# Convolution and two expert layers on one core: three blocks of tokens instead of two side by side in the first units

## The chip, the cores and the metric

The kernel runs on one core of a Trainium2 chip, in one launch. The metric is device time in microseconds (us), from the start to the end of the execution. Before the change the median of three runs is 2334.19 us (2333.78 to 2334.38). Engines: PE is TensorE (matmuls), DVE is VectorE, ACT is ScalarE, POOL is GpSimd, SP is SyncE, which here only issues DMAs.

## The reference

For 16384 tokens (4 sequences of 4096) of width 192, in float32:

```python
w = exp(weight - max) ; w = w / (sum(w) + 1e-9)      # 8 heads x 7 taps
out[b, s] = sum_k w[head, k] * x_pad[b, s + k]       # causal, 7 taps, 24 channels a head
h = maximum(out @ moe_w_in, 0); y1 = (h * h) @ moe_w_out        # 192 -> 2048 -> 192
h = y1 @ moe2_w_in; g = where(h > 0, h, exp(minimum(h, 0)) - 1); return g @ moe2_w_out
```

The weights of both layers come as float64 and are read as pairs of 32-bit words.

## The kernel before

**Blocks and units.** The tokens go in 32 blocks of 512 (TB). Layer 1 or 2 of a block is cut into 8 *units* of 256 hidden columns: `units` lists the 512 units as (layer, block, number). In the main loop, turn u issues the first products of unit u (`gemm1`: h, two PSUM banks) and the second products of unit u - 3 (`gemm2`, LAG = 3: they add to y, two banks, A for channels 0 to 127 and B for the other 64). Between them ACT takes `r` from h (`act_first`), squares it (layer 1) and rounds it to `gh`, and DVE (at some u POOL) computes the rest, `gl = r - gh` (`finish_lo`). Every operand is held as a high and a low part, so one logical product is three. `r` has two buffers, `gh` and `gl` three.

**Two forms of products.** From unit HALVES on, `products` issues the two halves of the array in turns (L458). Below it uses whole-array products (L471, L477): first those of h, then those of y.

**Order of the units.** `merge` lets layer 1 of block 0 begin at turn 0 and that of block 1 at turn 3, turn and turn about; then come layer 1 of blocks 2 and 3, layer 2 of blocks 0 and 1, and from there layer 2 of block j - 2 and layer 1 of block j. The first unit of block 1 is number 4, that of block 2 number 16.

**Weights.** A layer's weights are prepared in 18 pieces (`pieces`), each due at a unit. `piece_step` i ends piece i - 2 on POOL (`finish`), does the second part of piece i - 1 (DVE `power` and `rest`, POOL's sum) and the first part of piece i (ACT square, DVE `start`, `sign`, `guard`), and issues the load of a later piece, whose buffer `rest` has freed. So a step is five DVE operations (L178, L205, L189, L212, L200), and POOL does three or four for each piece. `more_pieces` makes up to two steps a unit as long as `begin[i] <= u`, with begin = due - 8 for layer 1.

**The convolution.** `place_x` brings a block into channel order: halo copies and two DVE transposes. For blocks 0 and 1 (`early`) the 7 taps are PE products with diagonal matrices (conv, 7 for half A of 512 columns, 7 for half B of 256; PE makes two passes of each), then `hi_a`, `hi_b` (ACT casts) and `lo_a`, `lo_b` (subtractions) make the four operand tiles X1[j]. For later blocks the taps are DVE operations (L349, L351). What isn't due at once stands in `bg`, from which `task` takes a few per unit, in order. All engines take their instructions in program order.

**PSUM.** `ps_h` has two buffers of two banks, `ps_y` four of one bank: two for y of each of two blocks; the early convolutions use `ps_y` too.

The pieces that the prediction's steps touch are `load_x`, `place_tasks`, `conv_tasks`, `gemm1`, `gemm2`, the list of units, and the block under `manual_schedule` ahead of the loop (the start).

Of the kernel before, what the change touches and what calls it, by code (L numbers as in the profile page):

```python
# [9 lines left out]
F32 = mybir.dt.float32  # L10
# [15 lines left out]

HALVES = 16

# [14 lines left out]
def conv_moe_moe_kernel(  # L43
# [39 lines left out]
    ev_p = ctx.enter_context(tc.tile_pool(name="ev", bufs=2))  # L83
    ps_h = ctx.enter_context(tc.tile_pool(name="ps_h", bufs=2, space=PSUM))
    ps_y = ctx.enter_context(tc.tile_pool(name="ps_y", bufs=4, space=PSUM))
# [24 lines left out]

    def softmax_taps():
# [149 lines left out]

    def load_x(j, second=nc.sync):
# [6 lines left out]
        def part(i, q):  # L269
            p = slice(q * Q, (q + 1) * Q)  # L270
            if i == 0:
                nc.sync.dma_start(out=a[p], in_=src[:, :, p])
            else:
                half, ch = q // 2, P + q % 2 * Q
                t = slice(half * (HB // Q), (half + 1) * (HB // Q))
                second.dma_start(out=b[p], in_=src[:, t, ch : ch + Q])
            if (i, q) == (1, P // Q - 1):
                xin[j] = (a, b)

        for i in range(2):  # L280
            for q in range(P // Q):
                later(lambda i=i, q=q: part(i, q))

    def place_tasks(j):
# [14 lines left out]
        def turn(i):  # L299
            while j not in xin:  # L300
                transfer()
            if i == 0:
                halo()
            t = xT[j][i]
            nc.vector.transpose(out=t[:, HALO:], in_=xin[j][i].rearrange("p t c -> p (t c)"))
            if i == 1:
                nc.vector.tensor_copy(out=t[DB:, 0:HALO], in_=t[0:DB, HB:])
                xin.pop(j)

# [3 lines left out]

        return [lambda: turn(0), lambda: turn(1), more]

# [21 lines left out]
    def conv_tasks(j, early=False):  # L337
        st = {}

        def tap(i, cw, k):  # L340
            t = xT[j][i]
            n = (TB, HB)[i]
            if early:
                if k == 0:
                    st[i] = ps_y.tile([P, TB], F32, tag="y", name=f"conv{i}")[:, 0:n]
                nc.tensor.matmul(st[i], diag(i, k), t[:, k : k + n], start=k == 0, stop=k == K - 1)  # L346
            elif k == 0:
                st[i] = acc_p.tile([P, n], F32, tag=f"acc{i}", name="acc")
                nc.vector.tensor_scalar(out=st[i], in0=t[:, 0:n], scalar1=cw[:, 0:1], scalar2=None, op0=ALU.mult)  # L349
            else:  # L350
                nc.vector.scalar_tensor_tensor(  # L351
                    out=st[i], in0=t[:, k : k + n], scalar=cw[:, k : k + 1], in1=st[i], op0=ALU.mult, op1=ALU.add
                )

        def hi_a():
            X1[j] = in_tiles("x1")
            nc.scalar.copy(out=X1[j][0], in_=st[0])

        def lo_a():
            eng = nc.gpsimd if j == 2 else nc.vector  # L360
            eng.tensor_tensor(out=X1[j][1], in0=st[0], in1=f32(X1[j][0]), op=ALU.subtract)
# [4 lines left out]
        def hi_b():  # L366
            for (p, n), (other, _) in zip(halves(), reversed(halves())):
                nc.scalar.copy(out=X1[j][2][p, n], in_=st[1][p, :])
                if j <= LEAD:
                    nc.scalar.copy(out=X1[j][2][other, n], in_=st[1][p, :])  # L370

        def lo_b():
# [3 lines left out]
            if j <= LEAD:  # L376
                for (p, n), (other, _) in zip(halves(), reversed(halves())):
                    nc.scalar.copy(out=l[other, n], in_=f32(l[p, n]))
                ready.add((1, j))
                return  # L380
# [11 lines left out]
        if early:  # L392
            return taps[0] + taps[1] + [hi_a, lo_a, hi_b, lo_b]
        return [t for both in zip(*taps) for t in both] + [hi_a, hi_b, lo_a, lo_b]
# [4 lines left out]

    def gemm1(W, X, i):  # L400


        h = ps_h.tile([P, 2, TB], F32, tag="h", name="h")
        work = {}
# [15 lines left out]
    def gemm2(layer, j, i, gh, gl):  # L420

        if i == 0:
            Y[layer, j] = [ps_y.tile([P, TB], F32, tag="y", name=f"y{layer}{s}") for s in "AB"]
        o = (W1 if layer == 1 else W2)["o"]
# [82 lines left out]
    def y1_tasks(j):  # L507
# [52 lines left out]

    units = merge((1, 0, 0, 1.0), (1, 1, LEAD, 1.0))
    phases = [(1, 2), (1, 3), (2, 0), (2, 1)]
    for j in range(4, NB):
# [48 lines left out]
    with tc.manual_schedule():  # L612
        nc.scalar.dma_start(out=taps[:, 0:K], in_=weight)
        load_piece()
        load_x(0, nc.scalar)
        for _ in range(2):
            load_piece()
        make_pick()
        diags.extend(in_tiles("x2", F32))
        make_identity(nc, diag(0, K))  # L620
        warm_up(4)
        softmax_taps()
        place_x(0)
        load_x(1)
        piece_step()
        spread_taps()
        warm_up(14)
        first, bg = conv_tasks(0, early=True), deque((0, t) for t in conv_tasks(1, early=True))
        for i, cw in enumerate((cwA, cwB)):
            make_diags(i, cw)  # L630
            for t in first[i * K : (i + 1) * K]:
                t()
            piece_step()
        place_x(1)
        load_x(2)
        for t in first[2 * K : 2 * K + 2]:
            t()
        piece_step()
        for t in first[2 * K + 2 :]:
# [22 lines left out]
        def next_x(l2, j2, c2):  # L662

            if (l2, j2) == (1, 1):
                return {0: 2, 3: 3}.get(c2)
            if l2 == 2 and c2 == 2 and j2 != 1:
                return 4 if j2 == 0 else j2 + 3 if j2 + 3 < NB else None

        for u in range(NU + LAG):
# [4 lines left out]
            if u < NU:  # L674
                layer, j, c = units[u]
                while (layer, j) not in ready:
                    bg.popleft()[1]() if bg else transfer()
                hs[u], first = gemm1(W1 if layer == 1 else W2, (X1 if layer == 1 else X2)[j], c)
            v = u - LAG
# [71 lines left out]
```

## Time and profile before

| | |
|---|---|
| median of 3 runs | 2334.19 us |
| profiled execution | 2334.18 us, its span 2332.5 us |
| PE busy | 2308.0 us, 19296 matmuls |
| DVE / ACT / POOL busy | 1720.6 / 1494.5 / 129.8 us |
| mean granted TensorE clock | 0.998 of full speed |
| HBM | 25.17 MB read, 12.58 MB written, 16 GB/s |

A busy PE is not PE at its peak, since matmuls overlap; where it waits is read from gaps and from the distance of the units. Of the 40 slices of the page PE shows less than 9 tenths only in the first and the last, and POOL works only in the first four: the weights are prepared there.

### The profile page before, as it was taken

The numbers are of one execution on the slowest core, as the hardware profiler recorded it, in microseconds if no ns is written. First come the engines' busy times: TensorE is split into PE (matmuls) and PEld (weight loads), VectorE is DVE, ScalarE is ACT, GpSimd is POOL, SyncE is SP. The second block draws the span as 40 slices with busy tenths as digits, with TensorE's granted clock in tenths as the row PEclk, the third lists the DMA queues.
The fourth block names the chain that finished last, engine by engine and source line by source line (L and its number), as shares of the span: only waits on it lengthen the run. The fifth ranks groups of instructions, "written<-read, shape, count | busy, mean of one in ns | idle before, by whom it ended". The sixth has DMA issues, their size and how long they took to land.

```text
span 2332.5 us, 46226 instructions
## 1 busy us (share of the span) xinstructions
PE 2308.0 (99%) x19296; PEld 2048.2 (88%) x19296; DVE 1720.6 (74%) x2032; ACT 1494.5 (64%) x1639; POOL 129.8 (6%) x149
## 2 busy tenths in 40 slices
PE   8899999999999999999999999999999999999998
PEld 6688998988998898888999899999989999988987
DVE  7978877767777777777777777677777777777665
ACT  5686756666666666666666666666666666666656
POOL 5465000000000000000000000000000000000000
PEclk9999999999999999999999999999999999999999
DMA  4211111000101000100001010001010001100000
GB/s 104 59 51 40 19 24 17 15 15 15 20 15 20 12 15 17 19 15 17 13 14 19 17 18 15 15 15 19 15 19 12 15 17 18 17 17 8 13 8 14
DMA packets 221342, 48.06 MB, mean 21 GB/s; under 512 B 206288, under 2 KB 219600, under 8 KB 221136
## 3 DMA queue, kind: packets, MB, share of 16 engines
q1 hardware_dynamic: 220032, 45.00, 10.1%
q8 instruction: 152, 2.49, 0.5%
q14 instruction: 54, 0.44, 0.1%
q10 hardware_dynamic: 1104, 0.13, 0.0%
HBM read 25.17 MB, written 12.58 MB: 16 GB/s over the span
## 4 chain that ended last, share of the span: by engine, by line
PE 94%; ACT 2%; DVE 2%; issue 1%; DMA 0%; POOL 0%; SPq 0%; DVEq 0%; ACTq 0%; POOLq 0%
PE h L458 43%; PE y2A L458 15%; PE y1A L458 14%; PE y1B L458 9%; PE y2B L458 9%; ACT gh L647 1%; DVE r L494 1%; ACT r L481 1%; PE h L471 1%; PE conv L346 1%; PE y1A L471 1%; ACT r L485 0%; PE h L477 0%; PE y1B L471 0%; DVE gl L653 0%
## 5 line engine op out<-in xcount | busy, mean ns | idle before, releaser
L647 ACT CAST gh<-r 128x1024 fp32r<-128x1024 f32 x512 | 538.1, 1051 | 632.9 <-DVE r L494 318.9
L653 DVE TENSOR_TENSOR gl<-r,gh 128x1024 fp32r<-128x1024 f32 x507 | 629.7, 1242 | 345.5 <-ACT gh L647 345.2
L481 ACT ACTIVATE r<-h 128x1024 f32<-128x1024 f32 x512 | 524.7, 1025 | 150.7 <-PE h L458 138.7
L458 PE MATMUL y2A<-gh,wo 64*128 64x512 f32 x2024 | 552.4, 392 | 0.0
L458 PE MATMUL y1A<-gh,wo 64*128 64x512 f32 x1944 | 531.2, 392 | 0.0
L494 DVE SCALAR_TENSOR_TENSOR r<-r,h 128x1024 f32<-128x1024 f32 x256 | 311.6, 1217 | 202.0 <-ACT r L485 176.5
L458 PEld LDWEIGHTS y2A<-gh,wo 64*128 64x128 f32 x2024 | 367.4, 184 | 21.7
L458 PEld LDWEIGHTS y1A<-gh,wo 64*128 64x128 f32 x1944 | 352.6, 184 | 13.1 <-issue 0.4
L458 PE MATMUL h<-x2Ah,wiAh 64*128 64x512 f32 x1024 | 326.4, 397 | 4.5 <-DVE r L494 4.5
L458 PE MATMUL h<-x2Al,wiAh 64*128 64x512 f32 x1024 | 323.2, 393 | 0.0
L458 PE MATMUL h<-x2Ah,wiAl 64*128 64x512 f32 x1024 | 322.1, 392 | 0.0
L458 PE MATMUL y2A<-gl,wo 64*128 64x512 f32 x1012 | 319.8, 395 | 0.0
L458 PE MATMUL y2B<-gh,wo 64*128 64x512 f32 x1012 | 314.2, 390 | 0.0
L458 PE MATMUL y2B<-gl,wo 64*96 64x512 f32 x1012 | 314.1, 390 | 0.0
L458 PE MATMUL y1A<-gl,wo 64*128 64x512 f32 x972 | 304.2, 392 | 0.0
L458 PE MATMUL h<-x1Ah,wiAh 64*128 64x512 f32 x960 | 302.7, 393 | 1.2 <-ACT r L481 1.2
L492 DVE SCALAR_TENSOR_TENSOR r<-h,r 128x1024 f32<-128x1024 f32 x224 | 272.6, 1217 | 41.8 <-ACT r L481 41.6
L458 PE MATMUL h<-x1Al,wiAh 64*128 64x512 f32 x960 | 302.7, 393 | 0.0
L458 PE MATMUL h<-x1Ah,wiAl 64*128 64x512 f32 x960 | 301.5, 391 | 0.0
L458 PE MATMUL y1B<-gh,wo 64*128 64x512 f32 x972 | 301.2, 389 | 0.0
L458 PE MATMUL y1B<-gl,wo 64*96 64x512 f32 x972 | 300.1, 388 | 0.4 <-POOL gl L653 0.4
L485 ACT ACTIVATE r<-r 128x1024 f32<-128x1024 f32 x256 | 271.6, 1061 | 8.1
(137 smaller groups left out, 4784.3 us busy)
## 6 DMA issues: line engine op xcount, KB each, us to landing
xinA<-in_x_dram SPq DMA_DIRECT2D x128, 64.0 KB, 2.2
out_dram<-zA SPq DMA_DIRECT2D x128, 64.0 KB, 2.0
raw<-in_moe_w_out_dram SPq DMA_DIRECT2D x16, 384.0 KB, 3.1
out_dram<-zB SPq DMA_DIRECT2D x64, 64.0 KB, 2.0
xinB<-in_x_dram SPq DMA_DIRECT2D x124, 32.0 KB, 1.9
x1Bh<-x1Bh SPq DMA_DIRECT2D x56, 64.0 KB, 1.9
x1Bl<-x1Bl SPq DMA_DIRECT2D x56, 64.0 KB, 1.9
raw<-in_moe_w_in_dram SPq DMA_DIRECT2D x8, 384.0 KB, 3.3
```

Source lines behind the costliest of these rows:

```text
L346: nc.tensor.matmul(st[i], diag(i, k), t[:, k : k + n], start=k == 0, stop=k == K - 1)
L458: m = nc.tensor.matmul(o, w[p], x[p], start=st, stop=sp)
L471: nc.tensor.matmul(o, w, x, start=st, stop=sp and part in ("A", "B"))
L481: nc.scalar.activation(out=r, in_=h, func=AF.Relu, scale=1.0 if layer == 1 else -1.0)
L485: nc.scalar.activation(out=r, in_=r, func=AF.Exp, scale=-1.0)
L492: nc.vector.scalar_tensor_tensor(out=r, in0=h, scalar=0.0, in1=r, op0=ALU.max, op1=ALU.mult)
L494: nc.vector.scalar_tensor_tensor(out=r, in0=r, scalar=-1.0, in1=h, op0=ALU.add, op1=ALU.max)
L647: nc.scalar.copy(out=gh, in_=gs[u])
L653: eng.tensor_tensor(out=gl, in0=gs.pop(u), in1=f32(gsplit[u][0]), op=ALU.subtract)
```

## The change

Three blocks are merged instead of two: block 0 begins at turn 0, block 1 at 2, block 2 at 4. So block 1's first unit is number 3, block 2's number 8, and blocks 0, 1 and 2 end layer 1 with units 15, 20 and 23. Three y need six banks: `ps_h` gets one buffer under each of two tags. Under tag "z" stand the convolution of block 0 and then y of block 0; until unit 19 (HALVES goes from 16 to 20) every h uses the one buffer "h", after that h alternates between the two. Block 2's convolution becomes PE products, and its operands use the second buffer of "x2". y of block 1 is taken up only after unit 23.

At the start the taps' softmax and x come ahead of the weights; half B is convolved before half A; two of x's eight loads go to ACT's queue; ACT's table is loaded early by a small exponential; the second warm-up has 8 products instead of 14.

```diff
-HALVES = 16
+HALVES = 20
...
-    ps_h = ctx.enter_context(tc.tile_pool(name="ps_h", bufs=2, space=PSUM))
+    ps_h = ctx.enter_context(tc.tile_pool(name="ps_h", bufs=1, space=PSUM))
...
+    def exp_table():
+        one = cpool.tile([H, 1], F32, name="one")
+        nc.vector.memset(one, 1.0)
+        nc.scalar.activation(out=one, in_=one, func=AF.Exp)
...
-        for i in range(2):
-            for q in range(P // Q):
-                later(lambda i=i, q=q: part(i, q))
+        for n, queue in enumerate(queues):
+            later(lambda i=1 - n // 4, q=n % 4, queue=queue: part(i, q, queue))
...
-        return [lambda: turn(0), lambda: turn(1), more]
+        return [lambda: turn(1), lambda: turn(0), more]
...
+        if early:
+            both = ps_h.tile([P, 2, TB], F32, tag="z", name="conv") if j == 0 else None
+            for i, n in enumerate((TB, HB)):
+                st[i] = (both[:, i] if j == 0 else ps_y.tile([P, TB], F32, tag="y", name=f"conv{i}"))[:, 0:n]
...
+        def begin_x1():
+            if j not in X1:
+                X1[j] = in_tiles("x2" if j == 2 else "x1")
...
-            return taps[0] + taps[1] + [hi_a, lo_a, hi_b, lo_b]
+            return taps[1] + [hi_b, lo_b] + taps[0] + [hi_a, lo_a]
...
-        h = ps_h.tile([P, 2, TB], F32, tag="h", name="h")
+        h = ps_h.tile([P, 2, TB], F32, tag=tag, name="h")
...
-            Y[layer, j] = [ps_y.tile([P, TB], F32, tag="y", name=f"y{layer}{s}") for s in "AB"]
+            if (layer, j) == (1, 0):
+                both = ps_h.tile([P, 2, TB], F32, tag="z", name="y10")
+                Y[layer, j] = [both[:, s] for s in range(2)]
+            else:
+                Y[layer, j] = [ps_y.tile([P, TB], F32, tag="y", name=f"y{layer}{s}") for s in "AB"]
...
+    def y1_from(j):
+
+        return at[1, 2, NP - 1] + 1 if j == 1 else 0
...
-    units = merge((1, 0, 0, 1.0), (1, 1, LEAD, 1.0))
-    phases = [(1, 2), (1, 3), (2, 0), (2, 1)]
+    units = merge((1, 0, 0, 1.0), (1, 1, 2, 1.0), (1, 2, 4, 1.0))
+    phases = [(1, 3), (2, 0), (2, 1)]
...
-        load_piece()
-        load_x(0, nc.scalar)
-        for _ in range(2):
-            load_piece()
+        exp_table()
+        softmax_taps()
+        load_x(0, (nc.sync,) * 6 + (nc.scalar,) * 2)
         make_pick()
         diags.extend(in_tiles("x2", F32))
         make_identity(nc, diag(0, K))
         warm_up(4)
-        softmax_taps()
+        for _ in range(3):
+            load_piece()
+        spread_taps()
         place_x(0)
         load_x(1)
...
+        warm_up(8)
+        for i, cw in ((1, cwB), (0, cwA)):
+            make_diags(i, cw)
+        first, bg = conv_tasks(0, early=True), deque()
+        later_x = conv_tasks(1, early=True) + place_tasks(2) + conv_tasks(2, early=True)
+        bg.extend((0, t) for t in later_x)
...
-                return {0: 2, 3: 3}.get(c2)
+                return {3: 3}.get(c2)
...
-                hs[u], first = gemm1(W1 if layer == 1 else W2, (X1 if layer == 1 else X2)[j], c)
+                hs[u], first = gemm1(W1 if layer == 1 else W2, (X1 if layer == 1 else X2)[j], c, "h" if u < HALVES or u % 2 else "z")
```

On PE, before, the second products of the first unit (y1A, y1B) are followed at once by the next unit's first products:

```order
L471 MATMUL y1B<-gh,wo_96 128x512 x2
L471 MATMUL y1B<-gl,wo_96 96x512 x2
L471 MATMUL h<-x1Ah,wiAh_92 128x512
L471 MATMUL h<-x1Ah,wiAl_93 128x512
L471 MATMUL h<-x1Al,wiAh_92 128x512
```

On PE, after, at the same place (y_455 is y of block 0 in the pair of banks, conv_199 the convolution of block 2's half B):

```order
L490 MATMUL y_455<-gh,wo_96 128x512 x2
L490 MATMUL y_455<-gl,wo_96 96x512 x2
L354 MATMUL conv_199<-xtB,x2Bh 128x256
L490 MATMUL h<-x1Ah,wiAh_92 128x512
L490 MATMUL h<-x1Ah,wiAl_93 128x512
```

A tap of block 2 now stands between the two, and it reads `xtB`, which DVE writes. On DVE, before, the third `gl` is followed by a piece step:

```order
L653 TENSOR_TENSOR gl<-r,gh 128x1024
L178 TENSOR_SCALAR a<-raw 128x384
L205 TENSOR_SCALAR m<-a 128x384
L189 SCALAR_TENSOR_TENSOR a<-raw,a 128x384
L212 SCALAR_TENSOR_TENSOR m<-raw,m 128x384
L200 SCALAR_TENSOR_TENSOR a<-m,a 128x384
```

On DVE, after, the placement of block 2 (halo copies, transposes) stands behind the third `gl`, ahead of the step:

```order
L680 TENSOR_TENSOR gl<-r,gh 128x1024
L299 COPY xtA<-xtA 128x6
L300 COPY xtB<-xtB 64x6
L309 STREAM_TRANSPOSE xtB<-xinB 128x256
L311 COPY xtB<-xtB 64x6
L309 STREAM_TRANSPOSE xtA<-xinA 128x512
L183 TENSOR_SCALAR a<-raw 128x384
```

That transpose is the one which the tap above reads. On DVE, after, between the sixth and seventh `gl` (first row) and the eighth to tenth (last row) stand a step and block 2's `lo_a`, `x2Al<-conv_198`:

```order
L680 TENSOR_TENSOR gl<-r,gh 128x1024 x2
L183 TENSOR_SCALAR a<-raw 128x384
L210 TENSOR_SCALAR m<-a 128x384
L194 SCALAR_TENSOR_TENSOR a<-raw,a 128x384
L217 SCALAR_TENSOR_TENSOR m<-raw,m 128x384
L205 SCALAR_TENSOR_TENSOR a<-m,a 128x384
L372 TENSOR_TENSOR x2Al<-conv_198,x2Ah 128x512
L680 TENSOR_TENSOR gl<-r,gh 128x1024 x3
```

This subtraction is what block 2's first unit, number 8, reads as its low part; before, block 2 had its taps and its subtractions later, ahead of unit 16.

## Rows read from the trace of the kernel before

**Rows 1.** The page, section 1: busy us (share), instructions.

```profile
PE 2308.0 (99%) x19296; PEld 2048.2 (88%) x19296; DVE 1720.6 (74%) x2032; ACT 1494.5 (64%) x1639; POOL 129.8 (6%) x149
```

**Rows 2.** Groups by line and form, ACT, 300 to 2300: busy us, mean ns, idle.

```profile
L481 ACT ACTIVATE r<-h 128x1024 f32<-128x1024 f32 x452 | 463.4, 1025 | 129.6 <-PE h L458 128.9
```

**Rows 3.** Busy time by window: PE, PEld, DVE, ACT, POOL, PE clock, DMA.

```profile
35.47:82.08 46.61, 38.34 (x163) 24.83 (x161) 46.52 (x65) 24.77 (x35) 35.49 (x38) 0.96 0.28 82
```

**Rows 4.** Waits of PE, 20 to 83: us in total, times, longest.

```profile
PE y1A L471 <- DVE gl L653: 5.2, 3, 2.4
```

**Rows 5.** Timeline of PE, 0 to 24: start us, us, line, tiles.

```profile
5.94 5.86 PE L335 MATMUL warm<-x2Al 128*128 128x128 f32 x28
...
20.49 0.58 PE L471 MATMUL h<-x1Ah,wiAh 128*128 128x512 f32 x1
...
23.78 0.49 PE L477 MATMUL h<-x1Bl,wiBh 64*128 64x512 f32 x2 [0.53 <-ACT x1Bl L378]
```

**Rows 6.** PE by window, block 0's A taps and B taps: length, busy.

```profile
11.64:17.65 6.01, 6.01 (x16) 1.00 0.45 119
17.65:20.49 2.84, 2.84 (x16) 1.00 0.68 108
```

**Rows 7.** Timeline of all engines, 0 to 45.

```profile
9.91 1.28 ACT L329 ACTIVATE x2Ah<-x2Al,cwA 128x128 f32<-128x128 f32 x4 [4.65 <-DVE cwA L126]
...
17.85 0.59 ACT L357 CAST x1Ah<-conv 128x512 fp32r<-128x512 f32 x1 [3.09 <-PE conv L346]
...
18.47 0.69 DVE L361 TENSOR_TENSOR x1Al<-conv,x1Ah 128x512 fp32r<-128x512 f32 x1 [1.19 <-ACT x1Ah L357]
```

**Rows 8.** Timeline of PE, 24 to 130: first products of units 9, 10, 15.

```profile
78.68 0.40 PE L471 MATMUL h<-x1Ah,wiAh 128*128 128x512 f32 x1
...
83.73 0.39 PE L471 MATMUL h<-x1Ah,wiAh 128*128 128x512 f32 x1
...
107.75 0.39 PE L471 MATMUL h<-x1Ah,wiAh 128*128 128x512 f32 x1
```

**Rows 9.** DVE by window: five pairs of steps, then a placement.

```profile
35.47:40.96 5.49, 5.49 (x11) 1.00 0.23 73
44.52:49.53 5.01, 5.01 (x11) 1.00 0.28 78
51.48:58.44 6.96, 6.96 (x12) 1.00 0.24 72
60.39:67.04 6.65, 6.65 (x11) 1.00 0.23 75
68.97:75.11 6.14, 6.14 (x12) 0.72 0.20 66
82.08:84.01 1.93, 1.84 (x6) 1.00 0.19 63
```

**Rows 10.** Timeline of DVE, 24 to 130.

```profile
33.95 1.59 DVE L653 TENSOR_TENSOR gl<-r,gh 128x1024 fp32r<-128x1024 f32 x1 [2.01 <-ACT gh L647]
...
43.63 0.86 DVE L375 TENSOR_TENSOR x1Bl<-conv,x1Bh 64x256 fp32r<-64x256 f32 x2
...
80.13 2.03 DVE L653 TENSOR_TENSOR gl<-r,gh 128x1024 fp32r<-128x1024 f32 x1
...
84.42 1.22 DVE L653 TENSOR_TENSOR gl<-r,gh 128x1024 fp32r<-128x1024 f32 x1
```

**Rows 11.** Windows with PE's granted clock (third last column).

```profile
68.00:70.00 2.00, 0.90 (x2) 0.78 (x3) 2.00 (x3) 0.20 (x1) 1.89 (x2) 0.80 0.39 144
70.00:72.00 2.00, 2.00 (x6) 1.43 (x5) 2.00 (x5) 2.00 (x3) 0.97 (x2) 0.50 0.00 0
72.00:74.00 2.00, 2.00 (x10) 1.31 (x11) 2.00 (x3) 1.16 (x2) 1.69 (x3) 0.85 0.58 188
```

**Rows 12.** The same view around two later waits.

```profile
142.00:146.00 4.00, 3.05 (x27) 2.31 (x23) 3.94 (x9) 2.10 (x4) 1.19 (x2) 1.00 0.01 2
...
220.00:222.00 2.00, 0.21 (x2) 0.00 (x0) 1.93 (x4) 0.21 (x1) 1.85 (x3) 1.00 0.00 0
```

More of the change, by code (lines that the diff above doesn't have):

```diff
@@ L260, in transfer, with load_x @@
         transfers.popleft()[1]()
-    def load_x(j, second=nc.sync):
+    def load_x(j, queues=(nc.sync,) * 8):
         a = xin_p.tile([P, TB // Q, Q], F32, tag="xinA", name="xinA")
@@ L267, in load_x, with part @@
         src = xf[j * TB : (j + 1) * TB, :].rearrange("(t p) d -> p t d", p=Q)
-        def part(i, q):
+        def part(i, q, queue):
             p = slice(q * Q, (q + 1) * Q)
             if i == 0:
-                nc.sync.dma_start(out=a[p], in_=src[:, :, p])
+                queue.dma_start(out=a[p], in_=src[:, :, p])
             else:
@@ L275, in part @@
                 t = slice(half * (HB // Q), (half + 1) * (HB // Q))
-                second.dma_start(out=b[p], in_=src[:, t, ch : ch + Q])
-            if (i, q) == (1, P // Q - 1):
+                queue.dma_start(out=b[p], in_=src[:, t, ch : ch + Q])
+            if (i, q) == (0, P // Q - 1):
                 xin[j] = (a, b)
-        for i in range(2):
-            for q in range(P // Q):
-                later(lambda i=i, q=q: part(i, q))
+        for n, queue in enumerate(queues):
+            later(lambda i=1 - n // 4, q=n % 4, queue=queue: part(i, q, queue))
     def place_tasks(j):
@@ L301, in turn @@
                 transfer()
-            if i == 0:
+            if i == 1:
                 halo()
@@ L343, in tap @@
             if early:
-                if k == 0:
-                    st[i] = ps_y.tile([P, TB], F32, tag="y", name=f"conv{i}")[:, 0:n]
                 nc.tensor.matmul(st[i], diag(i, k), t[:, k : k + n], start=k == 0, stop=k == K - 1)
@@ L353, in tap @@
                 )
+        def begin_x1():
+            if j not in X1:
+                X1[j] = in_tiles("x2" if j == 2 else "x1")
         def hi_a():
-            X1[j] = in_tiles("x1")
+            begin_x1()
             nc.scalar.copy(out=X1[j][0], in_=st[0])
         def lo_a():
-            eng = nc.gpsimd if j == 2 else nc.vector
-            eng.tensor_tensor(out=X1[j][1], in0=st[0], in1=f32(X1[j][0]), op=ALU.subtract)
+            nc.vector.tensor_tensor(out=X1[j][1], in0=st[0], in1=f32(X1[j][0]), op=ALU.subtract)
+            if early:
+                ready.add((1, j))
         def halves():
@@ L366, in hi_b @@
         def hi_b():
+            begin_x1()
             for (p, n), (other, _) in zip(halves(), reversed(halves())):
@@ L378, in lo_b @@
                     nc.scalar.copy(out=l[other, n], in_=f32(l[p, n]))
-                ready.add((1, j))
+                if not early:
+                    ready.add((1, j))
                 return
@@ L397, in in_tiles, with gemm1 @@
         return [in_p.tile([P, TB], dt, tag=f"{nm}{s}", name=f"{nm}{s}") for s in ("Ah", "Al", "Bh", "Bl")]
-    def gemm1(W, X, i):
-        h = ps_h.tile([P, 2, TB], F32, tag="h", name="h")
+    def gemm1(W, X, i, tag):
+        h = ps_h.tile([P, 2, TB], F32, tag=tag, name="h")
         work = {}
@@ L422, in gemm2 @@
         if i == 0:
-            Y[layer, j] = [ps_y.tile([P, TB], F32, tag="y", name=f"y{layer}{s}") for s in "AB"]
+            if (layer, j) == (1, 0):
+                both = ps_h.tile([P, 2, TB], F32, tag="z", name="y10")
+                Y[layer, j] = [both[:, s] for s in range(2)]
+            else:
+                Y[layer, j] = [ps_y.tile([P, TB], F32, tag="y", name=f"y{layer}{s}") for s in "AB"]
         o = (W1 if layer == 1 else W2)["o"]
@@ L621, in conv_moe_moe_kernel @@
         warm_up(4)
-        softmax_taps()
+        for _ in range(3):
+            load_piece()
+        spread_taps()
         place_x(0)
         load_x(1)
-        piece_step()
[L626 to L633, printed above, removed]
+        warm_up(8)
[4 more added lines that the diff above has]
+        bg.extend((0, t) for t in later_x)
+        for t in first[:K]:
+            t()
+        piece_step()
+        for t in first[K + 2 : 2 * K + 2]:
+            t()
+        piece_step()
+        for t in first[K : K + 2]:
+            t()
+        piece_step()
         place_x(1)
         load_x(2)
-        for t in first[2 * K : 2 * K + 2]:
-            t()
-        piece_step()
         for t in first[2 * K + 2 :]:
@@ L704, in conv_moe_moe_kernel @@
                     tasks = (y1_tasks if l2 == 1 else y2_tasks)(j2)
-                    bg.extendleft((0, t) for t in reversed(tasks))
+                    first_u = y1_from(j2) if l2 == 1 else 0
+                    bg.extendleft((first_u, t) for t in reversed(tasks))
                 jx = next_x(l2, j2, c2)
                 if jx:
-                    free = at[1, jx - 2, NP - 1] + 1
+                    free = at[1, 0 if jx == 3 else jx - 2, NP - 1] + 1
                     bg.extend((0, t) for t in place_tasks(jx))
```

## The prediction

> **What bounds the kernel now.** I read the page's busy shares first: TensorE (PE) is busy for 99% of the span [rows 1], so only PE time that is added or saved counts. Next the groups by line in the middle: the first activation of a unit stands 452 times in 2000 us, 4.43 us per unit [rows 2]; 512 units make 2268 us of the 2332.5, and the other 64 lie at the start, at some later waits and at the end. The change touches only units 0 to 23, so the start is what matters. There the windows show two stages. From 35.47 to 82.08 VectorE (DVE) is busy for 46.52 of 46.61 us and PE for only 38.34 [rows 3]: weight pieces and `gl` fill DVE's queue, and PE waits for `gl` [rows 4]. Later PE sets the pace: units 10 to 15 are 4.80 us apart ((107.75 - 83.73) / 5) [rows 8], in the whole-array form that holds below HALVES.
>
> **The sum's base.** Profiled execution 2334.18 us, equal to the median 2334.19; its span is 2332.5, with 1.7 outside. I follow the new order from the start to unit 20 and compare where unit 20 begins.
>
> **Step 1, the first unit comes earlier.** Before, its products start at 20.49 and the last pair ends at 24.27 [rows 5]. Now `pcw` still follows the first warm-up and ends at 6.0; 16 warm passes instead of 28 take 5.86 x 16 / 28 = 3.35, to 9.3 [rows 5]. Seven diagonals for the B half take about 2.25 (four took 1.28) [rows 7] and are done by then. The B taps take 2.84 and the A taps 6.01 [rows 6], to 18.2. Then the cast and subtraction of A, 0.59 and 0.69 [rows 7], with 0.3 of gaps: 19.8; the rest of the unit's products 1.9: 21.7. That is 2.6 us gained. The x loads move ahead of the weights on SP, and two of them to ACT's queue behind the exponential. I cost that at nothing: the B taps need x only at 9.3 and the A taps at 12.2, and the weight pieces that now come later are needed only at 19; if x came after 9.3, everything below would shift by that much.
>
> **Step 2, the first gl.** Behind unit 0 stand six B taps (2.84 x 6 / 7 = 2.4) instead of six A taps; unit 1's own products add half of 4.80: 26.5. Two ACT operations of about 1.03 lead to `gl` at 28.6 to 30.2, against 33.95 [rows 10]. Six piece steps stand ahead of it on DVE instead of seven.
>
> **Step 3, DVE's queue up to the third block.** Pairs of piece steps between two `gl` took 5.49, 5.01, 6.96, 6.65 and 6.14 us, and a `gl` among them 2.03 [rows 9, 10]; I use them in that order. After 30.2: `x1Bl` of block 1, 0.86 and 0.3 of waiting (31.4), a pair (36.9), `gl` (38.9), `x1Al` 0.69 (39.6) [rows 7, 10]. PE comes to unit 3, now block 1's first, at 35.1 (26.5 plus a B and three A taps, 3.0, unit 2, 2.4, four A taps, 3.4). It waits for `x1Al`; the unit ends 1.8 and 2.5 later, at 43.9. Its next instruction is block 2's first B tap. On DVE the transposes for it stand behind a pair and a `gl`: 39.6 + 5.0 + 2.0 = 46.6, and the B half's part of a placement that took 1.93 in all [rows 9] makes 47.4. PE idles 3.5 us there; behind that tap everything of PE waits.
>
> **Step 4, PE from there.** Units 4 to 7 take 4 x 4.80 = 19.2 [rows 8], block 2's fourteen taps 8.85 [rows 6]: 75.5. The single h buffer adds about 0.8 at unit 7, because the activation of unit 6 is queued on ACT behind block 2's `x1Bl` copies, which wait for DVE: 76.3. Elsewhere I price that buffer at nothing: 2.4 us of second products cover an activation of 1.03; without that cover it would cost 1.3 a unit. Block 2's convolution thus costs PE 8.85 us. What it takes off DVE stood before behind the placement of 82.08 to 84.01 [rows 9], where PE waited for nothing any more [rows 8], and saves nothing.
>
> **Step 5, DVE up to unit 8, the third block's first.** 46.6 + 1.9 (placement) + 6.96 + 2.0 + 6.65 + 2.0 + 0.86 (`x2Bl`) + 6.14 + 2.0 = 75.1. Then unit 7's activation, which waits for this `gl` because r has two buffers, `gh`, a `gl` of 1.2 to 2.0, one more step (half a pair, 3.1) and the subtraction, 0.69: 82.4. So DVE is late, not PE. Unit 8 needs that tile for its third product: 1.9 and 2.5 more, and unit 9 starts at 86.8. Before it started at 78.68 [rows 8]: 8.1 us later.
>
> **Step 6, four more units in whole-array form.** Now units 9 to 19 take 11 x 4.80 = 52.8: unit 20 at 139.6. Before: unit 10 at 83.73, six units of 4.80, four of 4.43: 130.3. That is 9.3 later.
>
> **Step 7, after unit 20.** Before, PE loses 0.95 us in 142 to 146 [rows 12], where block 3's subtractions crowd DVE. Now four tasks a unit run up to unit 19 and block 3 gets ahead, but y of block 0 must leave the bank pair before unit 20; I take back 0.8. Layer 2's steps keep their units, so the wait at 220 to 222 (PE busy 0.21 of 2) [rows 12] stays. Sum: 2334.2 + 9.3 - 0.8 = 2342.7; I say 2342.5.
>
> **Unknown costs and their bounds.** The new waits at units 3 and 8 were not there before: nothing (PE's own sum, rival C) to 3.5 and 5 us; I take the upper ends, since DVE shows no gap in rows 3. A DVE step costs between 2.5 and 3.5 us (half of 5.01 and of 6.96): eleven of them move unit 9 by about 5 us either way.
>
> **Rivals.** A: DVE gets through faster. `gl` took 2.03 beside a busy GpSimd and 1.22 beside an idle one [rows 10]; if all pairs cost 5.0, the last three save 4.75, the third block's tile is there at 77.7, and PE's own chain (76.3) nearly decides. Unit 9 starts at 82.1 and the sum is 2338. For it: DVE has waits in the new order, in which GpSimd catches up; against it: the same pieces stand on GpSimd. The Trainium skill, "SBUF — State Buffer", section "SBUF: two separate sides", says that DVE and GpSimd hold their shared port pair in turn, each for a whole instruction. By that rule the same pieces cost the same blocking, which lowers A's chance; the two `gl` durations agree with it.
>
> B: the clock. PE's granted clock was 0.50, the lower level of 1.2 GHz, in 70 to 72 [rows 11], after PE had waited 2.4 us for a `gl` [rows 4]. The windows beside it show 0.80 and 0.85, so the stretch lost 1.7 us. The new waits of 3.5 and 5 us are longer. A slow stretch behind the first is covered by DVE's lateness; one behind the second comes on top: 2344.2. If both count, 2346. The Trainium skill, "TensorE: Matmul & The Clock Gate", section "Why this matters for your kernels", asks for no idle gaps between bursts of matmuls, as the engine otherwise falls back to half rate. By that rule the sum would be 2344 or more; the trace agrees in this one place.
>
> C, faster: three blocks give PE work whenever a weight is late, and PE never waits up to unit 9. From 21.7 its own work is 2.4 + 2.4 + 3.0 + 2.4 + 3.4 up to unit 3, then 28.8 for six units and 8.85 for taps: unit 9 at 73, unit 20 at 125.8, 4.5 earlier than before; with the 0.95 lost in 142 to 146 [rows 12] gone too, 2328.7. It decides only if `x1Al` of block 1 is done by 35, block 2's transposes by 40 and its last subtraction by 70, that is, if DVE does the same pieces in three quarters of the time. Against it stands the full DVE of rows 3.
>
> D: the change does not do what it says, and the single h buffer parts the units instead: 1.3 us for each of the eleven units from 9 to 19 makes 14 more, 2357. Against it: the cover named in step 4.
>
> **Chances.** Forecast 0.52, A 0.22, B 0.14, C 0.08, D 0.04. This kernel's measurement tells about 0.2%, 4.7 us, from no change: faster is below 2329.5, slower above 2338.9. A falls mostly within it, as does the low edge of the forecast: faster 0.10, same 0.25, slower 0.65. Range 2334 to 2348: it leaves out C, D and the outer part of A; the forecast's own is 2339 to 2346.
>
> **What would show it.** Right: first activation near 21.8; PE idle at about 44 to 47 for block 2's first tap, waiting for DVE's transpose of xtB; PE idle at about 77 to 82 for `x2Al`; unit 9 near 87; 4.80 per unit up to unit 19. Wrong: PE without waits between 40 and 80 (C), no wait for `x2Al` (A), waits of `h` for the activation in each unit below 20 (D), or a second half of the kernel that runs at another pace than 4.43.

## The result, and the profile after

After the change the median is 2358.57 us (2358.14 to 2365.2, five runs), beside 2334.38 of the kernel before on the same chip; the ratio of after to before is 1.0109, 95% interval 1.0098 to 1.0119. It is slower, as forecast, but by 24 us and not by 8: 2358.57 lies outside the range of 2334 to 2348. The profiled span is 2356.8 us. All medians and ratios here are of the fast runs; one run each of e3 (3306 us) and e4 (2814 us) is left out as slow.

The page of the profile of after, section 1, and the groups by line of ACT in 300 to 2300 (busy us, mean ns, idle), to compare with [rows 1, 2]:

```profile
PE 2319.7 (98%) x19248; PEld 2004.7 (85%) x19248; DVE 1712.9 (73%) x2020; ACT 1492.8 (63%) x1640; POOL 126.0 (5%) x148
```

```profile
L500 ACT ACTIVATE r<-h 128x1024 f32<-128x1024 f32 x451 | 461.6, 1023 | 125.9 <-PE h L477 125.2
```

451 first activations in the same 2000 us where there were 452: the pace of the long middle is the same. All is lost early. To see where, I read the start of each unit's first activation (relu, L481 before, L500 after) from the timeline of ACT and cut the kernel into five stages. The table gives us, from one profiled execution of each kernel; the rows from e1 on are experiments, told below:

| kernel | start to unit 0 | unit 0 to 8 | 8 to 16 | 16 to 26 | 26 to 511 |
|---|---|---|---|---|---|
| before | 24.3 | 57.9 | 35.2 | 46.6 | 2155.5 |
| after | 31.3 | 62.1 | 38.4 | 57.1 | 2155.0 |
| e1 | 24.4 | 63.6 | 38.4 | 58.4 | 2156.1 |
| e2 | 31.0 | 61.9 | 38.4 | 53.9 | 2155.0 |
| e3 | 24.2 | 63.5 | 38.4 | 52.3 | 2155.8 |
| e5 | 24.3 | 63.5 | 38.4 | 49.4 | 2157.5 |
| e6 | 23.6 | 61.8 | 38.4 | 49.9 | 2157.5 |
| e7 | 23.6 | 61.8 | 38.4 | 48.4 | 2156.4 |
| e13 | 23.7 | 59.5 | 38.4 | 48.4 | 2155.8 |
| e4 | 22.0 | 60.7 | 36.6 | 46.6 | 2155.3 |
| e9 | 28.6 | 57.9 | 39.8 | 46.6 | 2154.6 |
| e14 | 23.3 | 57.9 | 34.1 | 48.2 | 2154.3 |

After loses 6.9 before unit 0, 4.2 up to unit 8, 3.3 up to unit 16 and 10.5 up to unit 26 (differences of the unrounded times), and nothing from there on, where before has a stretch at the slow clock (0.50 in 224 to 226) that after is spared.

**The start.** Timeline of ACT in after (start us, us, line, tiles, idle before and its releaser):

```profile
20.25 0.36 ACT L382 CAST x1Bh<-conv 64x256 fp32r<-64x256 f32 x1 [8.35 <-PE conv L354]
...
23.58 0.59 ACT L369 CAST x1Ah<-conv 128x512 fp32r<-128x512 f32 x1
...
31.29 1.02 ACT L500 ACTIVATE r<-h 128x1024 f32<-128x1024 f32 x1 [6.68 <-PE h L496]
```

The same of DVE, which shows what the late cast holds up:

```profile
21.78 0.88 DVE L389 TENSOR_TENSOR x1Bl<-conv,x1Bh 64x256 fp32r<-64x256 f32 x2 [8.34 <-ACT x1Bh L384]
...
26.85 0.69 DVE L372 TENSOR_TENSOR x1Al<-conv,x1Ah 128x512 fp32r<-128x512 f32 x1
```

Timeline of PE in after, which answers to [rows 5]:

```profile
7.10 3.76 PE L340 MATMUL warm<-x2Al 128*128 128x128 f32 x16 [0.94 <-DVE cwB L131]
10.65 2.26 PE L354 MATMUL conv<-xtB,x2Bh 128*128 128x256 f32 x8
12.74 1.46 PE L354 MATMUL conv<-xtB,x2Bl 128*128 128x256 f32 x6
...
17.47 2.74 PE L354 MATMUL conv<-xtA,x2Al 128*128 128x512 f32 x6
24.26 0.47 PE L490 MATMUL h<-x1Ah,wiAh 128*128 128x512 f32 x1 [4.05 <-issue]
...
27.60 0.79 PE L490 MATMUL h<-x1Al,wiAh 128*128 128x512 f32 x1 [2.63 <-DVE x1Al L372]
```

The B taps end at 14.2, but the cast that reads them, x1Bh, starts at 20.25, with the end of the last A tap (17.47 + 2.74). Behind it on DVE stand x1Bl, a weight step, block 1's placement and then x1Al, for which PE waits until 27.60. The windows show the clock as well (the third last column is PE's granted clock): PE had no product for 4.05 us ahead of 24.26, and in 27 to 30 the clock was 0.50, which is 1.2 GHz.

```profile
20.00:24.00 4.00, 0.21 (x1) 0.00 (x0) 2.16 (x7) 3.13 (x8) 0.07 (x1) 1.00 0.00 0
...
27.00:30.00 3.00, 2.40 (x6) 1.56 (x8) 3.00 (x8) 0.00 (x0) 1.04 (x2) 0.50 0.59 94
```

**From unit 0 to 16.** Waits of PE, 36 to 83 (us in total, times, longest), in place of [rows 4]; the first products of units 9 and 10, in place of [rows 8]; and the window of [rows 3]:

```profile
PE h L490 <- DVE x1Al L372: 2.9, 1, 2.9
PE conv L354 <- DVE xtB L311: 2.8, 1, 2.8
PE h L490 <- ACT x1Ah L369: 1.1, 1, 1.1
```

```profile
95.73 0.40 PE L490 MATMUL h<-x1Ah,wiAh 128*128 128x512 f32 x1
...
100.53 0.39 PE L490 MATMUL h<-x1Ah,wiAh 128*128 128x512 f32 x1
```

```profile
35.47:82.08 46.61, 39.79 (x150) 24.60 (x149) 43.14 (x67) 27.22 (x41) 31.22 (x35) 0.93 0.33 88
```

The first two waits are at the places that were forecast (x1Al at unit 3, then xtB for block 2's first tap, 2.8 where 3.5 was said); that for x2Al at unit 8 was 1.04, where 5 was said. Units 9 and 10 are 4.80 apart.

**Unit 20, the first in halves.** Timeline of all engines in after, 153 to 159:

```profile
155.21 2.47 POOL L680 TENSOR_TENSOR gl<-r,gh 128x1024 fp32r<-128x1024 f32 x1 [0.49 <-ACT gh L674]
155.40 2.70 DVE L217 SCALAR_TENSOR_TENSOR m<-raw,m 128x384 f32<-128x384 uint32 x1
...
158.17 0.38 SPq L162 DMA_DIRECT2D raw<-in_moe_w_out_dram  x1
...
158.66 0.79 PE L477 MATMUL y1A<-gh,wo 64*128 64x512 f32 x1 [5.18 <-SPq L482]
```

And from the waits of SP, 100 to 180 (us in total, times, longest):

```profile
SPq L162 <- DVE m L217: 4.0, 1, 4.0
```

In halves, the two halves of the array wait for each other through signals that SP passes on (L482). Ahead of unit 20's signal SP has a weight load (L162) that waits for DVE's last read of an older weight tile (L217); that read took 2.70 us beside GpSimd's gl. PE idles 5.18 us there.

### The profile page after: what moved, and what is told of

Its sections match the earlier page's. It is cut to its first block, busy times and chain, and to the rows that moved or that the text cites. A ratio compares the mean times of both kernels' runs of the same rounds, so it can differ in the third digit from the quotient of the medians.

```text
span 2356.8 us, 46098 instructions
## 1 busy us (share of the span) xinstructions
PE 2319.7 (98%) x19248; PEld 2004.7 (85%) x19248; DVE 1712.9 (73%) x2020; ACT 1492.8 (63%) x1640; POOL 126.0 (5%) x148
## 4 chain that ended last, share of the span: by engine, by line
PE 94%; DVE 3%; ACT 2%; issue 1%; POOL 0%; SPq 0%; DVEq 0%; POOLq 0%; ACTq 0%
PE h L477 42%; PE y2A L477 16%; PE y1A L477 15%; PE y1B L477 9%; PE y2B L477 8%; PE conv L354 1%; DVE r L513 1%; ACT gh L674 1%; PE h L490 1%; ACT r L500 1%; PE y L490 1%; PE h L496 1%; ACT r L504 0%; DVE gl L680 0%; DVE acc L359 0%
## 5 line engine op out<-in xcount | busy, mean ns | idle before, releaser
L500 ACT ACTIVATE r<-h 128x1024 f32<-128x1024 f32 x512 | 524.0, 1023 | 176.8 <-PE h L477 137.6
L477 PE MATMUL y1A<-gh,wo 64*128 64x512 f32 x1912 | 522.4, 392 | 5.2 <-SPq L482 5.2
L477 PEld LDWEIGHTS y1A<-gh,wo 64*128 64x128 f32 x1912 | 342.7, 184 | 23.0 <-SPq L482 5.6
L477 PE MATMUL y1A<-gl,wo 64*128 64x512 f32 x956 | 299.1, 393 | 0.0
L477 PE MATMUL y1B<-gl,wo 64*96 64x512 f32 (+1 forms) x956 | 296.6, 389 | 0.0
L477 PE MATMUL h<-x1Ah,wiAh 64*128 64x512 f32 x932 | 293.5, 393 | 0.0
L477 PE MATMUL h<-x1Ah,wiAl 64*128 64x512 f32 x932 | 293.0, 392 | 0.0
L477 PE MATMUL h<-x1Al,wiAh 64*128 64x512 f32 x932 | 292.9, 392 | 0.0
```

Source lines behind the costliest of these rows:

```text
L477: m = nc.tensor.matmul(o, w[p], x[p], start=st, stop=sp)
L500: nc.scalar.activation(out=r, in_=h, func=AF.Relu, scale=1.0 if layer == 1 else -1.0)
```

## The experiments

Each experiment has its median, with the ratio to the kernel before and its 95% interval; the kernel before, measured beside each, had medians of 2334.3 to 2335.0. The intervals are 4 to 8 us wide, so the stages of the table carry what the medians alone can't tell. One thing must be known to read them: of two kernels that are alike up to some unit, one can show a stretch at the lower clock ahead of it and the other not, which moves a stage by 1.7 us (told under e7).

**e1: a tile for each half of block 0's convolution.**

```diff
-            both = ps_h.tile([P, 2, TB], F32, tag="z", name="conv") if j == 0 else None
...
+                if j == 0:
+                    st[i] = ps_h.tile([P, 2, TB], F32, tag="zh"[i], name=f"conv{i}")[:, 0, 0:n]
```

> The changed kernel, with the two halves of block 0's convolution in two PSUM tiles instead of the two halves of one. Theory (the cast x1Bh reads only half B, done at 14.1 us, but waits for the last tap of half A at 20.2, because both lie in one tile): x1Bh starts at about 14.2 instead of 20.25, the step and the placement behind it fill DVE's gap of 8.34 us, x1Al is done at about 21.6 and the first activation stands at 23.5 to 24 instead of 31.29. DVE is the bound from there to unit 9, so all of it carries: about 7.5 us less than the changed kernel, near 2351. Rival 1 (the cast waits for the taps themselves, in PE's order, whatever tile they write): x1Bh still at 20.25, time within 1 us of the changed kernel. Rival 2 (the start is made up later, where PE waits for weights anyway): first activation at 24, but unit 20 earlier by less than 3 us, time 2355 to 2358.

2355.61, 1.0087 (1.0072 to 1.0102). Timeline of ACT in e1:

```profile
14.92 0.37 ACT L384 CAST x1Bh<-conv 64x256 fp32r<-64x256 f32 x1 [3.03 <-PE conv L356]
...
24.43 1.03 ACT L502 ACTIVATE r<-h 128x1024 f32<-128x1024 f32 x1 [2.46 <-PE h L498]
```

The cast starts right behind the B taps and unit 0 is 6.9 us earlier: the tile is the cause, and rival 1 falls. Of the 6.9, 5.4 are left at units 8 and 16 and 4.9 at unit 20's activation, more than rival 2 allowed. But unit 20's wait is still there (5.2), more time at the slow clock stands behind it (told under e3), and the whole gains only 3.0: the theory's 2351 was missed, and the time is in rival 2's range by another way.

**e2: weight loads held back from unit 16.**

```diff
-        if HALVES <= now < NU:
+        if 16 <= now < NU:
```

> The changed kernel, with the weight loads held back (issued two units later) from unit 16 on instead of 20, so that the load that SP took up just before unit 20's signals stands behind them. Theory (PE's wait of 5.18 us in unit 20 is SP standing at that load, which waits for DVE's last read of an older weight tile): the wait goes; GpSimd's gl that ends at 157.68 is then the next thing late, by about 1.5 us, so 3.5 to 4 us less, near 2354.5. Rival 1 (that gl, or DVE, is what unit 20 and 21 wait for anyway): 0 to 1 us less. Rival 2 (the load held back is itself late, and a weight piece of layer 2 comes late for it): no gain or a loss of some us.

2355.50, 1.0089 (1.0073 to 1.0106). PE's waits in 140 to 170:

```profile
PE h L490 <- ACT r L500: 1.8, 1, 1.8
PE y1B L477 <- POOL gl L680: 1.6, 1, 1.6
```

The wait for SP is gone and GpSimd's gl is late by 1.6, as the theory had it; unit 20 comes 5.2 earlier and the trace as a whole is 3.7 shorter.

**e3: both.**

> Both edits together (two tiles for block 0's convolution, weight loads held back from unit 16). If the two losses are separate, the gains add: 7.5 + 3.5 to 4 = 11 us less than the changed kernel, near 2347.5, and what stays against the kernel before is block 2's convolution on PE (8.85 us), the four more units in whole-array form (1.5) and the waits of units 17 to 19. Rival (an earlier start only moves the wait of unit 20 to another load, since SP's queue fills with another timing): the sum is that of the split alone, 2351.

2349.08 (three runs), 1.0062 (1.0045 to 1.0079): 9.5 less than after, against 3.0 and 3.1 for the parts; it lies between the theory's 2347.5 and the rival's 2351. The parts give less because slow clock stands behind the wait that each leaves: 155 to 160 at 0.61 in e1 and at 0.75 in e2, while e3 shows 1.00 from 150 to 163, with the same wait for gl as in e2. Over the windows around these waits a clock below 1.00 took (estimate: length times what is missing to 1.00) 1.7 us in after, 3.4 in e1, 1.7 in e2 and nothing in e3. That is 3.4 more for the pair than the sum of the parts; the spans of the profiles give 3.0 more (9.7 against 3.0 and 3.7). The first row is of e1, the second of e3.

```profile
155.00:160.00 5.00, 5.00 (x30) 3.84 (x29) 0.47 (x1) 2.46 (x3) 1.32 (x2) 0.61 0.06 23
```

```profile
155.00:160.00 5.00, 5.00 (x46) 4.42 (x44) 4.42 (x7) 4.52 (x5) 3.62 (x3) 1.00 0.30 84
```

**e5, e6, e7: units 16 to 20.** On top of e3, e5 queues block 3's tasks five units earlier, e6 takes gl of units 15 and 18 off GpSimd, e7 does both:

```diff
-                return {3: 3}.get(c2)
+                return {1: 3}.get(c2)
...
-            eng = nc.gpsimd if u in range(15, 30, 3) else nc.vector
+            eng = nc.gpsimd if u in range(21, 30, 3) else nc.vector
```

> The kernel with both edits (e3), with block 3's placement and taps put into the task queue from block 1's second piece on instead of its fourth (five units earlier). In e3, DVE is busy for 1.4 of 5 us in 90 to 100, and then units 16 to 19 take 21.4 us where the kernel before takes 14.2: 7.1 us lost. Theory (the loss is DVE's queue: four taps a unit beside weight steps, up to unit 19): with the taps in DVE's empty stretch, units 16 to 19 take 15 to 17 us; what stays is GpSimd's gl of units 15 and 18 (ACT waits 3.4 us for it). 4 to 6 us less than e3's 2349.5, near 2344.5. Rival 1 (the single h buffer parts these units whatever DVE does): units 16 to 19 still take over 20 us, 0 to 1 less. Rival 2 (the taps now delay gl in units 9 to 13): each gl 1 to 2 us late, no gain.

> e3 with gl of units 15 and 18 on DVE instead of GpSimd (the third of each three goes to GpSimd from unit 21 on). Theory (GpSimd's 2.5 us for a gl, for which ACT's next activation waits 3.4 us in units 17 to 20 and PE 1.6, is the larger part of the loss in units 16 to 19): 3 to 4 us less than e3, near 2346. Rival (DVE's full queue is the cause, and two more subtractions of 1.2 to 2 us in it cost what they give): within 1 us of e3.

> e3 with both: block 3's tasks five units earlier and gl of units 15 and 18 on DVE. If the two causes are separate, units 16 to 19 take about 14.5 us as in the kernel before (4.80 a unit at the pace of whole-array form), 7 us less than e3: near 2342.5, which is what the prediction said for the whole change. Rival (the single h buffer): still over 18 us for these three units, 2346 or more.

e5 2347.70, 1.0052 (1.0037 to 1.0067); e6 2345.66, 1.0048 (1.0033 to 1.0063); e7 2345.04, 1.0042 (1.0028 to 1.0056). By the stage from unit 16 to 26, e5 takes 49.4 us, e6 49.9 and e7 48.4, where e3 takes 52.3: each cause is real, 2.9, 2.5 and together 3.9. The times tell less. Some 2.3 us of e6's and e7's distance to e3 arise ahead of unit 9, where the edits do nothing: 0.6 ahead of unit 0, and 1.7 because e3 has a second stretch at the slow clock there (0.76 in 50 to 55 and 0.90 in 55 to 60) where e6 and e7 have 1.00. And e5 and e6 give 1.7 back behind unit 26 (2157.5) by a longer slow stretch (0.50 in 234 to 240 of e5). So e5 missed its expected 2344.5, and e6 met its 2346 by luck. e7's profiled execution, 2343.3, is the quickest of its five (up to 2345.3). PE in 136 to 141, e3 first, then e7:

```profile
136.00:141.00 5.00, 3.25 (x15) 2.31 (x14) 2.44 (x4) 3.63 (x7) 1.80 (x2) 1.00 0.19 52
```

```profile
136.00:141.00 5.00, 5.00 (x25) 3.23 (x24) 3.41 (x7) 4.21 (x8) 0.00 (x0) 1.00 0.00 0
```

With both, the three units from 16 to 19 take 16.2 us; 14.5 was expected, and e7's 2342.5 was missed by its median. But PE waits for nothing there, and rival "single h buffer" (over 18 us) falls.

**e8: no middle taps for block 2** (so what it computes for that block is something else).

```diff
+            if early and j == 2 and 0 < k < K - 1:
+                return
```

> e3 without the five middle taps of either half of block 2's convolution on PE (taps 1 to 5 are left out, so block 2's result is another one); about 6.3 us of PE's work go (5/7 of 8.85), no task of another engine moves in its queue. Step 5 of the prediction (DVE is late for block 2's last subtraction, not PE): unit 9's activation moves from 92.5 by less than 2 us, time 2347.5 to 2349.5. Rival (PE's own chain sets unit 9, since DVE shows 2 us of idle time in 75 to 80 of e3): unit 9 near 86.5 to 87.5, time 5 to 6 us less, near 2344.

2350.17, 1.0065 (1.0050 to 1.0080): with 6.3 us of PE's work gone, unit 9's activation stands at 92.9, in e3 at 92.5. PE's free time became waits and slow clock (0.72 in 80 to 92, e3 1.00). From the waits of PE in e8, 40 to 92:

```profile
PE h L494 <- DVE x2Al L376: 1.8, 1, 1.8
```

In e3 that wait is 1.3. So the tile from DVE, and not PE's own work, sets unit 8, as step 5 said. That unit 9 did not move at all is partly the clock: x2Al ended 2.1 us sooner than in e3 (83.42 and 85.50), and the products behind it ran slowly.

**e13: block 2 enters at unit 12** (e7 otherwise).

```diff
-    units = merge((1, 0, 0, 1.0), (1, 1, 2, 1.0), (1, 2, 4, 1.0))
+    units = merge((1, 0, 0, 1.0), (1, 1, 2, 1.0), (1, 2, 6, 1.0))
```

> The repaired form (e7) with block 2 entering four units later (offset 6 instead of 4 in the merge: its first unit is number 12 instead of 8). In e7, PE waits 2.4 us for block 2's cast and subtraction at unit 8, 4.1 us for those of block 1 at unit 3 and 2.1 us for block 2's first tap. Theory (step 5: block 2's tile, behind the weight steps on DVE, is what unit 8 and 9 wait for): these 2.4 us go, time about 2343. Rival (DVE's weight steps themselves set units 7 to 9; a unit of block 0 or 1 in place of block 2's first wants a weight piece or a gl as late): 0 to 0.5 less, or some us more, since blocks 0 and 1 then ask for the next weights sooner.

2340.57, 1.0031 (1.0019 to 1.0042). The waits for block 2's tile are gone and unit 8 comes 2.2 us sooner, near the theory's 2.4; the profiled span is 2.8 shorter, and the median 4.5 lower, as e7's profiled execution was a quick one.

**e4: the new start alone, in the kernel before** (the start block, the loads' order and half B first, as in the change's diff; each half of the convolution keeps a tile of its own, and h its two buffers).

```diff
-        load_piece()
-        load_x(0, nc.scalar)
...
+        exp_table()
+        softmax_taps()
+        load_x(0, (nc.sync,) * 6 + (nc.scalar,) * 2)
...
-        warm_up(14)
+        warm_up(8)
```

> The kernel before, with the new start alone: exponential table and softmax first, x before the weights, half B before half A, eight warm passes instead of fourteen, each half of the convolution in a tile of its own; two blocks side by side, HALVES 16, two buffers for h as before. If the start as such is a gain, as step 1 of the prediction had it: first activation at 21.8 to 22.5 instead of 24.35, time 1.9 to 2.6 us less than before, near 2332. Rival (the placement of block 1 now stands on DVE ahead of the subtraction x1Al, and the taps end no earlier than the weights allow): first activation at 23.5 to 24, 0 to 0.8 less. Rival 2 (the loss of the changed kernel's start lies in the new order of loads and steps itself, not in the tile): first activation at 28 or later, 2338 or more.

2335.95, 1.0006 (0.9996 to 1.0015): no change. The taps run at 9.18 to 18.4 and the first activation at 22.01, as step 1 worked out; but unit 8 is at 82.69, before at 82.25. DVE, full in both in this window (29.80 of 30 us in before), takes it all back. e4:

```profile
60.00:90.00 30.00, 23.31 (x93) 14.59 (x92) 29.79 (x42) 15.00 (x18) 19.77 (x21) 0.94 0.30 79
```

The first activation came as expected, but both expectations of a gain in time fell: an early unit 0 is worth nothing there.

**e9: one buffer for h below unit 16, in the kernel before** (from there on h alternates between two tags, as in the change).

```diff
-    ps_h = ctx.enter_context(tc.tile_pool(name="ps_h", bufs=2, space=PSUM))
+    ps_h = ctx.enter_context(tc.tile_pool(name="ps_h", bufs=1, space=PSUM))
```

> The kernel before with one buffer for h up to unit 15 instead of two (from unit 16 on two in turn, as in the changed kernel), and nothing else. Step 4 of the prediction (the second products of a unit, 2.4 us, cover the activation of 1.03): 0 to 2 us more, 2335 to 2337, and units 9 to 15 still 4.4 to 4.8 apart. Rival D (the single buffer parts the units, 1.3 us for each of them): 9 us more for units 9 to 15 alone, 2344 or more.

2343.71, 1.0038 (1.0024 to 1.0052): not step 4's 0 to 2 us. The time is about rival D's, the mechanism another. 4.3 us are lost ahead of unit 0: the warm-up, in the same one buffer as the tap sums (pcw), waits for cwB. And 4.5 by the activations of units 8 and 12. Units 9 to 12 are 4.80 apart, so no unit is parted by 1.3. But PE can no longer run ahead while ACT's activation waits for DVE: it waits for ACT's r five times at units 4 to 8, 11.6 us in all. In before, unit 9's products stood at 78.68 and its activation at 85.73, and with that lead units 8 to 12 could be activated 3.4 apart. PE, timeline of e9:

```profile
10.19 5.89 PE L335 MATMUL warm<-x2Al 128*128 128x128 f32 x28 [4.02 <-DVE cwB L126]
...
67.22 0.80 PE L471 MATMUL h<-x1Ah,wiAh 128*128 128x512 f32 x1 [3.98 <-ACT r L481]
...
82.53 0.50 PE L471 MATMUL h<-x1Ah,wiAh 128*128 128x512 f32 x1 [0.58 <-ACT r L481]
...
87.56 0.50 PE L471 MATMUL h<-x1Ah,wiAh 128*128 128x512 f32 x1
```

The last two rows are units 8 and 9: unit 9 starts 8.9 us later than in [rows 8], so both losses are in by then.

**e11, e14: HALVES at 20 alone, without and with the loads held back, in the kernel before.** In e14 also e2's edit.

```diff
-HALVES = 16
+HALVES = 20
```

> The kernel before with HALVES at 20 instead of 16: the whole-array form, four background tasks a unit and the immediate loads reach to unit 19, and nothing else. Step 6 of the prediction (four units at 4.80 instead of 4.43): 1.5 us more, 2336. Rival (what was lost in units 16 to 20 of the changed kernel, 7 us of crowding and 5.2 us at SP's load, belongs to this constant alone, not to three blocks): 6 to 13 us more, 2341 to 2347.

> The kernel before with HALVES at 20 and the loads held back from unit 16 on, as in e2. Theory (the whole-array form itself costs 0.37 us in each of four units): PE's wait of 4.5 us for SP's signal in unit 20 goes, 1.5 us more than before, 2336.5. Rival (the four tasks a unit and gl one unit later cost something too): 3 to 5 us more, 2338 to 2340.

e11 2340.35, 1.0022 (1.0013 to 1.0032); e14 2332.73, 0.9994 (0.9985 to 1.0004). PE in e11:

```profile
139.76 0.79 PE L458 MATMUL y1A<-gh,wo 64*128 64x512 f32 x1 [4.49 <-SPq L463]
```

So the wait at SP belongs to the constant and the load order, not to three blocks: e11's rival (2341 to 2347) came nearer than its theory (2336). Without the wait, the four units in whole-array form cost 0.5 in sum, where step 6 had 1.5: 1.6 more in the stage from 16 to 26 and 1.1 less in the one ahead of it. Both expectations for e14 were too high.

**e10, e12: can the kernel before be bettered?** e10 has e6's edit (gl of units 15 and 18 on DVE); e12 also this:

```diff
-HALVES = 16
+HALVES = 12
```

> The kernel before with gl of units 15 and 18 on DVE instead of GpSimd, the edit that gave the changed kernel's repaired form 3.8 us. Before, PE is busy for 3.82 and 4.58 of 5 us in 145 to 155, and a gl of GpSimd is among its waits there with 0.4 us only. Theory (the loss in units 16 to 19 came with block 3's tasks and the whole-array form reaching to unit 19 together; here DVE has room): 0 to 1 us less, 2334. Rival (GpSimd's gl costs this kernel too): 2 to 4 us less, 2331 to 2333, which would beat both kernels.

> The kernel before with HALVES at 12 and gl of unit 15 and 18 on DVE: four units fewer in whole-array form. If a unit in halves is worth 0.37 us also there: 1.5 us less, 2333. Rival (DVE, busy for 4.7 to 5 of 5 us up to 100, falls behind when gl is wanted in the same unit): same or 1 to 3 us more.

e10 2334.55, 0.9998 (0.9988 to 1.0007); e12 2336.94, 1.0010 (1.0001 to 1.0020), 2 us more, as its rival had it. By e10 GpSimd's gl costs nothing where DVE isn't crowded. No kernel tried is clearly faster than before; e14 comes nearest, with 1 inside its interval.

## Why the prediction was wrong

The miss of 16.0 us is made of four parts: unit 0 later by 9.6 than forecast; from there to unit 9's first product 0.7 better; from that to unit 20's first 2.1 worse (54.9, forecast 52.8); the remaining 5.0 behind unit 20's start, where PE waited 5.18.

The two steps that failed are 1 and 7.

**Step 1 failed.** "Now `pcw` still follows the first warm-up ... 21.7 ... 2.6 us gained" was worked out as if each half were free on its own, and the tiles and buffers that it goes through were priced at nothing. In e4, where it is, the number holds (22.01). In the change it met two things, both in the diff and neither priced. The two halves share one tile, so the first reader waits for the last writer: 6.9 us (e1). And the warm-up shares the one h buffer with the tap sums and waits for cwB, which is made from them: it begins at 7.1 in e1 and at 5.9 in e4, the taps at 11.1 and 9.2, and the first activations are 2.4 apart. That the gain would last was wrong too, at least in the kernel before (e4).

**Steps 2 to 5 held as differences, in part by luck.** From unit 0's activation to unit 9's first product there were 64.4 us, forecast 65.1. On the way two misses made up for each other: block 2's first tap came 28.9 us behind unit 0's activation (forecast 25.7), and then DVE was quicker, since the last three pairs of steps took 17.8 us and not 19.75. xtB made PE wait 2.8 (3.5), and DVE, not PE, was late for block 2 (e8, e13). The wait at x2Al was 1.04 and not 5, as PE came late itself, after slow-clock products at unit 0 and at unit 3. (By step 3's own terms PE comes to unit 3 at 35.3, not 35.1; nothing hangs on it, as x1Al was set at 39.6.)

**Step 6 held in size**: 4.80 a unit up to unit 18's start; then rival D showed once, 1.76 us of PE for ACT's r at unit 19, behind DVE's and GpSimd's crowd (e5, e6). From unit 9 to unit 20 that made 54.9 for 52.8.

**Step 7 failed.** "I take back 0.8": instead the stage from unit 16 to 26 lost 10.5. It looked at block 3's tasks as something that "gets ahead", not at what four tasks a unit do to DVE while GpSimd holds a gl for 2.5 us (3.9, e7 against e3), and it did not follow SP's queue across the new first unit in halves (3.2 of that stage from after to e2, 6.1 from e1 to e3, both with the slow clock behind the wait). SP's load orders had been counted at the start, but not at unit 20. The Trainium skill, "DMA: Bandwidth & Descriptors", section "Anatomy of one DMA — SWDGE (gpsimd) path", says that a transfer's semaphore wait is spent on the issuing engine's sequencer; the SP rows agree (4.0 us at L162), and the case adds what stood behind it.

**Rivals.** B's mechanism was there, as a consequence: 0.50 at unit 0, at unit 3 (50 to 54) and after unit 20's wait. D came near in time (2357), for other reasons, which is chance; in the kernel before its buffer costs some 4 at the start and 4 up to unit 12 by itself (e9), of which step 4 priced 0.8. In the change step 5's lateness of DVE may cover part of the second (argued, not measured), so these don't add to the rest. A came in part: the last three pairs took 17.8 us, forecast 19.75, A 15.0; the late start outweighed it. C fell: PE waited at units 3 and 8 and for block 2's first tap.

With the three losses mended (e7) the median is 2345.0, the stages of its profile +3.9, +3.3 and +1.8 over before, and block 2 entering later (e13) brings 2340.6. That the forecast of 2342.5 lies between the two does not bear it out: e7 has edits of its own, and its unit 9 is activated 4.5 us later than before, where step 5 had 8.1. Left open: why one execution has a second slow stretch ahead of unit 8 (e1, e3, e5) and another not (e6, e7); and how much of e9's 4.5 is in the change itself, since two h buffers beside six y banks would be ten banks, where these kernels use eight, and weren't tried.

## What to carry to other kernels

Before pricing a reordered start, list for each tile who writes it last and who reads it first: a reader of one half waits for the writer of the other if they share a tile, and a pool cut to one buffer ties together tiles that never met before. Follow each in-order queue, the one that only issues transfers too, across every place where the form of the work switches; a load that waits for a buffer there holds back each signal behind it. And a gain ahead of a full engine can be taken back by it, as by DVE in e4: price a stage by the engine that is full in it.

## What the runs showed of the hardware

- The same DVE instruction on 128x384 took 0.55 us once in the kernel before (row below, its L212) and 2.70 us in after, begun 0.19 us behind a GpSimd subtraction of 2.47: it ended 0.42 us after that one. Here the meeting cost 2.15 us on the way of a load, some four times the instruction alone.

```profile
24.14 0.55 DVE L212 SCALAR_TENSOR_TENSOR m<-raw,m 128x384 f32<-128x384 uint32 x1
```

- A wait of PE did not always bring a slow clock. After 5.18 us the granted clock was 0.50 in 159 to 161 of after. A wait of 2.86 us that ended at 223.07 in before was followed by 0.50 in 224 to 226; the same wait in after, 2.85 us to 247.99, by 1.00. After 1.62 us for gl the clock was 0.53 in 159 to 161 of e2, and after 1.61 us it stayed at 1.00 in e3, though both had waited 1.75 us for ACT's r 12 us earlier. What decides is not shown. By the estimate under e3 it accounts for two repairs of 3.0 and 3.1 us that gave 9.5 together. The window of after:

```profile
159.00:161.00 2.00, 2.00 (x12) 1.50 (x12) 0.00 (x0) 0.00 (x0) 1.86 (x4) 0.50 0.69 197
```
